# Two score tiles a quad shared between ScalarE and VectorE in the last full attention layer

## The chip, the cores and the metric

The kernel runs on one core of one Trainium2 chip. The metric is the device time of one execution in microseconds, the median of several runs. A profile of one execution shows what each engine did: TensorE (PE, its weight loads as PEld), VectorE (DVE), ScalarE (ACT), GpSimd (POOL) and the DMA queue of SyncE (SP).

## The reference

Four attention layers follow each other on x of 2048 rows by 512 columns, in float32. Layers 0 and 2 look back over a window of 256 rows, layers 1 and 3 over all rows; the two windowed layers have one set of weights, the two full ones another. Each layer is

```
x = x + attention(layernorm(x)) @ wo
```

with 32 heads of 16 columns. For a full layer:

```python
scores = jnp.einsum("bhqd,bhkd->bhqk", q, k) * Dh ** -0.5
p = softmax(scores, axis=-1)
o = jnp.einsum("bhqk,bhkd->bhqd", p, v)
```

So a full layer has 32 x 2048 x 2048 exponentials.

## The kernel before, in words

**Tiles.** Attention works on a quad: four heads and 512 queries (QC). In a full layer a quad goes through 16 steps j (NT), each of 128 keys, and in each step through two pairs of heads (pr). For one pair, `exps` (L755) issues eight matmuls of 64x32 array tiles that write a score tile `s` of 128 keys x 2 heads x 512 queries in PSUM, two banks, one for each head. The pool has two such tiles. One ScalarE instruction (L772) takes exp(SCALE x s) of both banks, 1024 elements a partition, into a tile `e` in SBUF, of which there are six. There is no maximum to subtract: a shift is worked into extra rows of queries and keys.

The function `pv` inside `attn_full` (L813) multiplies the exponentials with the values: four heads times two halves of the 128 keys (r), each half adding into its own accumulator bank `acc[r]`, head h in its partitions from 32 h on. The values carry a column of ones, so that row DH of an accumulator is the sum of the exponentials, by which `epilogue` (L718) divides. The profile lists two matmul records for each of these float32 matmuls.

**Order.** On PE and, in the full layers, on VectorE the order of the instructions is that in which the program emits them. ScalarE and GpSimd get theirs from the framework. `attention` (L1025) runs the generator `attn_full` and emits, for each step j: the scores and exponential of pair 0; then, at `flush(1)`, what waits in `pvq`, which is the value product of the step before the last; then the scores and exponential of pair 1; then, at `sd.step()`, a piece of side work. At the end of a quad the order differs: in step 0 of the next quad the value products of steps 14 and 15 are emitted, one after each pair, and the epilogue follows; step 1 has no value product.

Layer 3 runs over four groups t of eight heads, in each over four blocks c of 512 queries, in each over two quads: 32 quads. V is kept in tiles for half the heads and half the keys.

**Side work.** Projections of keys and queries (K3, Q3), values (VV) and the output projection (O3) of layer 3 run beside the attention in pieces of two matmul groups, dealt out by `Side.share` (L988). It keeps a budget, which grows with each step by the work that is left over the steps that are left, and a lag, which grows with PE time given to side work and falls by 0.42 a step. A piece is emitted if the lag is below 0.25 or the budget above 0.45. All is planned while the program is built, against a clock of its own (`spent`, `vec`); nothing of it happens on the chip. The results of side work come into one pair of PSUM banks and are joined on VectorE (`join`, L425). The squares of keys and queries are formed on GpSimd (L534) and summed on PE (L556).

**VectorE's queue.** Operations of VectorE that can wait go into four queues `VQ`, in order of precedence, and `drain` (L237) emits from the first that has something whenever the planned time of VectorE (`vt_`) is not ahead of the planner's clock by more than 0.2.

**Names that the change touches.** `PH`, the state of the phase (L212); `VQ` (L214); `exps` and its ScalarE instruction (L772); `attn_full` with `pv` (L805 to L820); and the loop in `attention` from L1059 to L1080. The tags "xh" (four buffers) and "st" (two buffers) belong to the normalisations, which have no work in layer 3.

Of the kernel before, what the change touches and what calls it, by code (L numbers as in the profile page):

```python
# [9 lines left out]
F32 = mybir.dt.float32  # L10
# [3 lines left out]
I32 = mybir.dt.int32  # L14
AF = mybir.ActivationFunctionType
ALU = mybir.AluOpType
AX = mybir.AxisListType

S, D, H, DH, WIN = 2048, 512, 32, 16, 256
P = 128  # L20
NT = S // P
# [3 lines left out]
QC = 512  # L25
# [5 lines left out]
SCALE = DH ** -0.5  # L31
MM = 0.222
HEAD_START = 100
PIECE = 4
EB, XB, XNB, WB, VB, OB = 6, 4, 4, 2, 3, 5
RINGS = WB, VB
L_MIN = 2.0 ** -90
L_SUM = 2.0 ** 60
WS = 16.0
W_MIN, W_MAX = 2.0 ** -7, 4.0  # L40


# [148 lines left out]
def fast_path(ctx, tc, flag, a_x, a_wqkv, a_wo, b_wqkv, b_wo, out):  # L191
# [3 lines left out]
    nc = tc.nc  # L195
# [3 lines left out]
    vp = pool("work", 2)  # L199
# [9 lines left out]
    mats = {(ty, s): layers[ty][1][:, s * D:(s + 1) * D] if s < 3 else layers[ty][2]  # L209
            for ty in range(2) for s in range(4)}  # L210

    XC, XN, V, O, OT, KM, PH = {}, {}, {}, {}, {}, {}, {"free": 0.0, "busy": False}  # L212
    WT, ST, pend = {}, {}, []
    VQ, vt_ = [deque() for _ in range(4)], [0.0]  # L214

    clock, DONE, XNR, ONR = [0.0], {}, {}, {}

    def spent(us):
        clock[0] += us
        return us  # L220
# [5 lines left out]
    def vec(us):  # L226

        vt_[0] = max(vt_[0], clock[0]) + us
# [39 lines left out]
    acc = [ps_c.tile([P, QC], F32, name=f"acc{i}") for i in range(2)]  # L268
# [52 lines left out]
    def split(ty, s, raw):  # L321

        w = wp.tile([P, NC, 2, D], F16, name=f"w{ty}_{s}", tag="vf", bufs=NQ)
        for k in range(NC):
            nc.scalar.activation(w[:, k, 0], raw[:, k], AF.Copy, scale=WS)
            nc.vector.scalar_tensor_tensor(w[:, k, 1], raw[:, k], WS, w[:, k, 0], op0=ALU.mult, op1=ALU.subtract)
            yield
# [96 lines left out]

    def join(dst, ps, scale=1 / WS):  # L425

        vec(1.4)
        nc.vector.tensor_scalar(dst, ps[0], scale, None, op0=ALU.mult)  # L428
        nc.vector.scalar_tensor_tensor(dst, ps[1], scale, dst, op0=ALU.mult, op1=ALU.add)  # L429
# [61 lines left out]
    def project(l, s, c, act, ht=None, ring=0):  # L491
# [13 lines left out]
        for t in range(NHT) if ht is None else (ht,):  # L505
# [5 lines left out]
            with tc.high_priority(HEAD_START):  # L511
# [4 lines left out]
                else:  # L516
                    sp = vp.tile([P, 2, QC], F16, name=f"sp{n}_{t}", tag="sp", bufs=3)
                    if act:
                        nc.scalar.activation(sp[:, 0], ps, AF.Copy, scale=1 / WS)
                    else:  # L520
                        nc.vector.tensor_scalar(sp[:, 0], ps, 1 / WS, None, op0=ALU.mult)
                    nc.vector.scalar_tensor_tensor(sp[:, 1], ps, 1 / WS, sp[:, 0], op0=ALU.mult, op1=ALU.subtract)
            full = PH["full"]
# [82 lines left out]
    def settle(all_=True):  # L606
        while pend and (all_ or pend[0][0] <= clock[0]):
            pend.pop(0)[1]()
# [143 lines left out]
        if u:  # L752
            soon(1, 1.2, parts)

    def exps(name, kt, qt, pr, pieces):  # L755

        ps = ps_s.tile([P, 2, QC], F32, name=f"s{name}", tag="s")
        w0 = min(p[3] for p in pieces)
        w1 = max(p[3] + p[2] for p in pieces)
        for kc, qc, wd_, s0 in pieces:  # L760
            if PH["full"]:
                for g in range(0, P, 32):
                    for h in range(2):
                        nc.tensor.matmul(ps[g:g + 32, h], kt[R * h:R * h + R, pr, kc + g:kc + g + 32],  # L764
                                         qt[R * h:R * h + R, pr], start=True, stop=True, skip_group_check=True)
                continue
            for h in range(2):
                nc.tensor.matmul(ps[:, h, s0:s0 + wd_], kt[R * h:R * h + R, pr, kc:kc + P],  # L768
                                 qt[R * h:R * h + R, pr, qc:qc + wd_], start=True, stop=True)
        spent(0.27)  # L770
        e = pp.tile([P, 2, QC], F32, name=f"e{name}", tag="e", bufs=EB)
        nc.scalar.activation(e[:, :, w0:w1], ps[:, :, w0:w1], AF.Exp, scale=SCALE)  # L772
        return e

    def flush(n):
# [27 lines left out]
        return kt, qt  # L803

    def attn_full(l, c, qd, kt, qt, a):  # L805
        for j in range(NT):
            es_ = []
            for pr in range(2):
                es_.append(exps(f"{l}_{c}_{qd}_{j}_{pr}", kt[j // 8], qt, pr, [(j % 8 * P, 0, QC, 0)]))
                if pr == 0:  # L810
                    yield None

            def pv(j=j, es_=es_):  # L813
                for h in range(4):
                    for r in range(2):
                        k = slice(R * r, R * r + R)
                        nc.tensor.matmul(acc[r][32 * h:32 * h + DH + 1, :], V[l, qd // 4, j // 8][k, j % 8, 4 * (qd % 4) + h, :],  # L817
                                         es_[h // 2][k, h % 2, :], start=(j == 0), stop=(j == NT - 1),
                                         skip_group_check=True)
            yield pv  # L820


# [99 lines left out]
    class Side:  # L922
# [13 lines left out]
        def one(self, force=False):  # L936

            drain()
            if PH["busy"]:
                return self.piece(PH["last"])  # L940
            if force:
                self.prefetch()
            at = [(w.ready_at(), i) for i, w in enumerate(self.q)]
            at = [(r, i) for r, i in at if r is not None]
            now = [i for r, i in at if r <= clock[0]]
            if now:
                i = now[0]
            elif force:
                r, i = min(at)
                clock[0] = r  # L950
            else:
                return None
            PH["last"] = self.q[i]
            return self.piece(PH["last"])
# [70 lines left out]
    def attention(l, works):  # L1025

        win = l % 2 == 0
        phase(l)
        load = load_win if win else load_full
        sd = None  # L1030
        for t in range(NHT if l == 3 else 1):
            for c in range(NQ):
                qds = range(2 * t, 2 * t + 2) if l == 3 else range(NQD)
                if l == 1:

                    sd = sd or Side(NT * NQD // 2, works[0], works[1], 0.33)
                    while ("Q", 1, c) not in DONE or pend and PH["busy"]:
                        sd.one(True)
                    settle()
                else:  # L1040
                    sd = Side((3 if win else NT) * len(qds), works[t * NQ + c], works[t * NQ + c + 1], 0.34 if l == 3 and t < 2 else 0.0)
                ahead = deque([PRE.pop("w", None) or load(l, c, qds[0])])
                if win:
                    ahead.append(load(l, c, 1))
                for qd in qds:
                    if (l, c, qd) == (1, 0, NQD // 2):
                        sd.finish()
                        sd = Side(NT * NQD * NQ - NT * NQD // 2, works[1], works[2], 0.33)
                    while (l, c, qd % 2) == (1, 0, 1) and qd + 1 in qds and ("S", 1, (qd + 1) // 2) not in DONE:
                        if ("K1", (qd + 1) // 2) in DONE and not PH["busy"]:  # L1050
                            settle()
                        else:
                            sd.one(True)
                    ops = ahead.popleft()
                    if qd + 1 + win in qds:
                        ahead.append(load(l, c, qd + 1 + win))
                    a = acc[qd % 2 if win else 0]
                    began, u = clock[0], 0
                    for f in (attn_win if win else attn_full)(l, c, qd, *ops, a):  # L1059
                        drain()  # L1060
                        if f is None:
                            flush(1)
                            if u == 1:
                                sd.step()
                            continue
                        clock[0] = max(clock[0], began + (2.4 if win else 1.8))
                        began = clock[0]
                        pvq.append([f])
                        if win:
                            flush(2)  # L1070
                            sd.step()
                            settle(False)
                        elif u == 0:
                            flush(1)
                        elif u:
                            sd.step()
                        while not win and (c, qd, u) == (0, 0, NT - 5) and ("V", l, 3, (0,), 2) not in DONE:
                            sd.one(True)
                        drain()
                        u += 1  # L1080
                    pvq[-1].append(lambda l=l, c=c, qd=qd, a=a: epilogue(l, c, qd, a))
                if l != 1 or c == NQ - 1:
                    sd.finish(l == 3 and (t, c) != (NHT - 1, NQ - 1))
                if not win and not PH["busy"]:
                    settle()
        flush(0)
        drain(4)
        phase(None)
# [151 lines left out]
    late = lambda l: [("N", l, 3)]  # L1240
# [56 lines left out]
```

## Time and profile before

| | |
|---|---|
| time, median of 3 runs | 2690.12 us (2688.55 to 2694.06) |
| time of the profiled execution | 2692.26 us |
| its span | 2690.2 us |
| ACT busy | 2363.6 us, 88% |
| PE busy | 2474.9 us, 92% |
| DVE busy | 1107.5 us, 41% |
| POOL busy | 531.8 us, 20% |
| exponentials, L772, of 128x1024 | 2368, mean 1066 ns |
| value products of the full layers, L817 | 16384 records, mean 590 ns |
| scores of the full layers, L764 | 16384 records, mean 381 ns |
| granted TensorE clock | 0.991 |

How to read it. Busy time counts an instruction from its start to its end, and instructions on one engine overlap: matmuls of different array tiles run at once and their ends are modelled, and an exponential begins before the one ahead of it has left the engine. So busy shares and mean durations are not rates. The rate at which an engine gets through its work is read from the starts of its instructions, in the timeline. A row of the timeline has the start, the duration, the engine, the line and operation, what is written from what with the shape, how many instructions are merged in it, and in brackets the idle time of the engine just before, with what ended it.

The first exponential of layer 3 starts at 1709.22 us, the last at 2669.2 us; from 1731.6 us on they follow each other with little idle time.

### The profile page before, as it was taken

What the parts mean: (1) busy time and instruction counts of PE and PEld (TensorE: products, weight loads), DVE (VectorE), ACT (ScalarE), POOL (GpSimd) and SP (SyncE); (2) the same over time, 40 slices, a digit from 0 to 9 for tenths busy, and PEclk for the clock granted to TensorE, in tenths of its full rate; (3) what the DMA queues carried; (4) which work ended last, traced back from release to release, by engine and by line L of the source; (5) the groups of instructions that cost most, each with busy time, mean ns of one, the idle gap of its engine ahead of it and who ended that gap; (6) DMA issues with size and microseconds to landing.
All of it is one profiled execution on the core that took longest, in us unless ns stands there. A gap on an engine that the chain in (4) does not pass through costs nothing.

```text
span 2690.2 us, 120844 instructions
## 1 busy us (share of the span) xinstructions
PE 2474.9 (92%) x54767; PEld 1133.5 (42%) x54767; DVE 1107.5 (41%) x2350; ACT 2363.6 (88%) x2671; POOL 531.8 (20%) x1072
## 2 busy tenths in 40 slices
PE   7889999999998999999999999899999999999997
PEld 3344444444443444444444444544444443433332
DVE  5576453223334434434236666232333323333333
ACT  4666764999999999999996776699999999999997
POOL 1556550000000100100116886010000000000000
PEclk9999999999999999999999999999999999999999
DMA  8889875232334325324227666433333323334332
GB/s 281 254 274 268 236 198 155 69 97 86 110 94 120 97 91 148 103 87 115 92 77 211 189 171 166 128 95 105 98 97 97 106 77 114 106 98 126 126 118 93
DMA packets 341189, 361.29 MB, mean 134 GB/s; under 512 B 117800, under 2 KB 256568, under 8 KB 334392
## 3 DMA queue, kind: packets, MB, share of 16 engines
q1 hardware_dynamic: 340664, 353.46, 44.2%
q8 instruction: 430, 7.05, 1.1%
q14 instruction: 95, 0.78, 0.1%
HBM read 240.65 MB, written 96.99 MB: 126 GB/s over the span
## 4 chain that ended last, share of the span: by engine, by line
ACT 55%; PE 23%; issue 11%; DVE 6%; DMA 3%; SPq 1%; POOL 0%; ACTq 0%; DVEq 0%; POOLq 0%
ACT e L772 55%; PE b L406 7%; PE acc L850 4%; PE acc L817 3%; PE s L764 2%; PE s L768 2%; PE bs L409 2%; PE b L409 2%; PE b L402 1%; DMA kt<-kw 1%; DVE xh L461 1%; DVE xn L455 0%; DMA qs<-sp 0%; SPq L483 0%; DVE xh L455 0%
## 5 line engine op out<-in xcount | busy, mean ns | idle before, releaser
L772 ACT ACTIVATE e<-s 128x1024 f32<-128x1024 f32 (+2 forms) x2432 | 2241.6, 1056 | 143.2 <-PE s L768 104.5
L817 PE MATMUL acc<-e,vt 64*17 64x512 f32 x16384 | 1094.6, 590 | 1.9 <-issue 1.9
L764 PE MATMUL s<-qt,kt 64*32 64x512 f16 x16384 | 860.0, 381 | 123.9 <-ACT e L772 97.1
L764 PEld LDWEIGHTS <-kt 64*32 64x32 f16 x16384 | 408.2, 89 | 935.1 <-issue 853.8
L817 PEld LDWEIGHTS acc<-e,vt 64*17 64x17 f32 x16384 | 283.8, 92 | 67.9 <-issue 8.1
L843 POOL TENSOR_SCALAR_AFFINE_SELECT e<-e 128x256 f32<-128x256 f32 x512 | 230.5, 457 | 154.8 <-ACT e L772 154.1
L840 POOL TENSOR_SCALAR_AFFINE_SELECT e<-e 128x256 f32<-128x256 f32 x448 | 201.5, 456 | 96.5 <-ACT e L772 93.2
L850 PE MATMUL acc<-e,vt 128*17 128x384 f32 (+2 forms) x2816 | 202.6, 390 | 2.5 <-POOL e L840 2.2
L749 POOL TENSOR_TENSOR oh<-o,oh 128x512 f16<-128x512 f32 x31 | 36.1, 1165 | 725.1 <-DVE oh L748 725.1
L428 DVE TENSOR_SCALAR sa<-acc 128x512 f32<-128x512 f32 x64 | 44.3, 691 | 291.3 <-PE acc L817 291.3
L406 PE MATMUL b<-xc,w 128*32 128x512 f16 x2496 | 152.4, 389 | 10.8 <-DVE km L575 6.9
L714 DVE SCALAR_TENSOR_TENSOR x<-b,x 128x512 f32<-128x512 f32 x122 | 84.0, 689 | 175.1 <-PE b L402 168.4
L534 POOL TENSOR_TENSOR sq_h<-sp_h 128x512 bf16<-128x512 f16 x29 | 43.0, 1483 | 562.4 <-DVE sp_h L528 562.4
L768 PE MATMUL s<-qt,kt 64*128 64x384 f16 (+2 forms) x1408 | 120.8, 276 | 28.2 <-ACT e L772 22.7
L534 POOL TENSOR_TENSOR sq<-sp 128x512 bf16<-128x512 f16 x32 | 45.8, 1434 | 496.8 <-DVE sp L528 473.6
L402 PE MATMUL b<-xc,w 64*32 64x512 f16 x3072 | 126.4, 376 | 1.5 <-DVE j L429 0.8
L428 DVE TENSOR_SCALAR vt<-b 128x256 f32<-128x256 f32 (+1 forms) x36 | 18.4, 512 | 233.8 <-PE b L402 219.9
L402 PE MATMUL b<-wo,oh 64*32 64x512 f16 x2592 | 109.1, 376 | 4.1 <-DVE m_None L591 1.8
L402 PE MATMUL b<-xc,w_h 64*32 64x512 f16 x2784 | 111.8, 376 | 0.1
L428 DVE TENSOR_SCALAR j_h<-b 128x512 f32<-128x512 f32 x29 | 20.1, 692 | 214.6 <-PE b L402 214.6
L406 PEld LDWEIGHTS <-w 128*32 128x32 f16 x2496 | 73.5, 99 | 79.2 <-issue 27.7
L768 PEld LDWEIGHTS <-kt 64*128 64x128 f16 x1408 | 52.2, 94 | 125.7 <-issue 105.3
(142 smaller groups left out, 1942.3 us busy)
## 6 DMA issues: line engine op xcount, KB each, us to landing
kt<-kf SPq DMA_DIRECT2D x128, 512.0 KB
qt<-qs SPq DMA_DIRECT2D x128, 256.0 KB
xd<-x SPq DMA_DIRECT2D x96, 256.0 KB
x<-xd SPq DMA_DIRECT2D x96, 256.0 KB
w<-wd SPq DMA_DIRECT2D x21, 1024.0 KB
kt<-kw SPq DMA_DIRECT2D x64, 256.0 KB
qs<-sp SPq DMA_DIRECT2D x48, 256.0 KB
wo<-wd SPq DMA_DIRECT2D x12, 1024.0 KB
```

The source lines that it names most:

```text
L402: nc.tensor.matmul(ps[g:g + 32, r], a[k, g:g + 32], b[k], start=(i == 0), stop=(i == len(pairs) - 1), skip_group_check=True)
L406: nc.tensor.matmul(ps[g:g + 32], a[:, g:g + 32], b, start=(i == 0), stop=(i == len(pairs) - 1), skip_group_check=True)
L409: nc.tensor.matmul(ps, a, b, start=(i == 0), stop=(i == len(pairs) - 1))
L534: nc.gpsimd.tensor_tensor(sq, sp[:, 0], sp[:, 0], ALU.mult)
L714: nc.vector.scalar_tensor_tensor(xs[i], p, 1 / WS, xs[i], op0=ALU.mult, op1=ALU.add)
L764: nc.tensor.matmul(ps[g:g + 32, h], kt[R * h:R * h + R, pr, kc + g:kc + g + 32], qt[R * h:R * h + R, pr], start=True, stop=True, skip_grou ...
L768: nc.tensor.matmul(ps[:, h, s0:s0 + wd_], kt[R * h:R * h + R, pr, kc:kc + P], qt[R * h:R * h + R, pr, qc:qc + wd_], start=True, stop=True)
L772: nc.scalar.activation(e[:, :, w0:w1], ps[:, :, w0:w1], AF.Exp, scale=SCALE)
L817: nc.tensor.matmul(acc[r][32 * h:32 * h + DH + 1, :], V[l, qd // 4, j // 8][k, j % 8, 4 * (qd % 4) + h, :], es_[h // 2][k, h % 2, :], star ...
L840: nc.gpsimd.affine_select(v, v, pattern=[[0, 2], [-1, P]], compare_op=ALU.is_gt, fill=0.0, base=0, channel_multiplier=1)
L843: nc.gpsimd.affine_select(v, v, pattern=[[0, 2], [1, P]], compare_op=ALU.is_ge, fill=0.0, base=0, channel_multiplier=-1)
L850: nc.tensor.matmul(a[32 * h:32 * h + DH + 1, q * P:(q + nb) * P], V[l, (4 * c + j) // 4][:, j % 4, 4 * qd + h, :], es_[h // 2][:, h % 2, s ...
```

## The change

In layer 3 alone, the second pair's score tile of steps j = 4 and j = 9 of each quad is shared by two engines. ScalarE takes the exponential of one bank; the other bank (bank 1 in step 4, bank 0 in step 9: `OWN`) goes to VectorE. `own_exp` reads it from PSUM, scaled to a power of two in fixed point, splits it by two bit operations into an integer and a fractional part, and evaluates a polynomial of five `scalar_tensor_tensor` steps, in float32 tiles with the tag "xh". The framework is told that the two reads of the tile need no order between them. The first operation is emitted at once; the seven others go into a new fifth queue of VectorE, `VQ[4]`, the last in precedence.

The result is twice the exponential, so the values of these two heads and key tiles are halved, on GpSimd, at the start of each quad (`vh`, tag "st"). The value product of a shared head is left out of its step's `pv`, and the products of both shared heads are emitted together by `late`, four matmuls, after the second pair's scores of step 15, ahead of that step's side work. Before them `late` emits whatever is left in `VQ[4]`. The planner counts 0.86 for them on its clock and on the lag.

```diff
+OWN = {4: 1, 9: 0}
+POLY = (-0.2122642642036666, 20.582234973412888, 57.43304580516819, 188.4105936388931, 265.3878017523131)
+OWN_AT = 13
+LEAD, LOW = 0x40000000 | 0x761904, -117.0
...
-    VQ, vt_ = [deque() for _ in range(4)], [0.0]
+    VQ, vt_ = [deque() for _ in range(5)], [0.0]
...
+    def own_exp(name, s, got, other):
+        u, e, p = (vp.tile([P, QC], F32, name=f"{n}{name}", tag="xh", bufs=XNB) for n in ("ou", "oe_", "op_"))
+        ui, ei = u.bitcast(I32), e.bitcast(I32)
+        with tc.high_priority(HEAD_START):
+            x = nc.vector.tensor_scalar(ui, s, SCALE * 1.4426950408889634 * 2.0 ** 23, LOW * 2.0 ** 23, op0=ALU.mult, op1=ALU.max)
+            tc.declare_no_dep(x.ins, other.ins, reason="the two read different banks")
+        vec(0.75)
+        ops = [(0.45, lambda: nc.vector.tensor_scalar(ei, ui, 0x7F800000, LEAD, op0=ALU.bitwise_and, op1=ALU.bitwise_xor)),
+               (0.45, lambda: nc.vector.tensor_scalar(ui, ui, 0x7FFFFF, 0x3E800000, op0=ALU.bitwise_and, op1=ALU.bitwise_or))]
+        for i, k in enumerate(POLY):
+            ops.append((0.7, lambda i=i, k=k: nc.vector.scalar_tensor_tensor(p, p if i else u, k / 4.0 ** (i + 1), e if i == 4 else u,
+                                                                            op0=ALU.add, op1=ALU.mult)))
...
+        for us, f in ops:
+            VQ[4].append((clock[0] + 0.6, us, lambda f=f: one(f)))
+        return p
...
-        nc.scalar.activation(e[:, :, w0:w1], ps[:, :, w0:w1], AF.Exp, scale=SCALE)
+        if own is not None:
+            x = nc.scalar.activation(e[:, 1 - own], ps[:, 1 - own], AF.Exp, scale=SCALE)
+            got[name] = own_exp(name, ps[:, own], got, x)
+        else:
+            nc.scalar.activation(e[:, :, w0:w1], ps[:, :, w0:w1], AF.Exp, scale=SCALE)
...
     def attn_full(l, c, qd, kt, qt, a):
+        got = {} if l == 3 else None
+        if l == 3:
+            vh = [vp.tile([P, 4, 6], F32, name=f"vh{l}_{c}_{qd}_{x}", tag="st").rearrange("p a b -> p (a b)")[:, :DH + 1] for x in range(2)]
+            for x, (j, own) in enumerate(OWN.items()):
+                nc.gpsimd.tensor_scalar(vh[x], V[l, qd // 4, j // 8][:, j % 8, 4 * (qd % 4) + 2 + own, :], 0.5, None, op0=ALU.mult)
...
+                mine = OWN if l == 3 else {}
+                for h in range(4):
+                    if j not in mine or h != 2 + mine[j]:
+                        head(j, h, es_[h // 2][:, h % 2], j == NT - 1)
+                def late():
+                    while got["left"]:
+                        vec(VQ[4][0][1])
+                        VQ[4].popleft()[2]()
+                    for x, (i, own) in enumerate(mine.items()):
+                        head(i, 2 + own, got[f"{l}_{c}_{qd}_{i}_1"], False, vh[x])
+                    spent(0.86)
+                if j == OWN_AT and mine:
+                    PH["late"] = late
...
                         elif u:
+                            if PH["late"]:
+                                PH["late"]()
+                                PH["late"] = None
+                                sd.lag += 0.86
                             sd.step()
```

`head(j, h, e, last_, v)` issues the two matmuls (one for each half of the keys) of head h, as `pv` did before. `OWN_AT` is 13 because the `pv` of step 13 is emitted in step 15.

More of the change, by code (lines that the diff above doesn't have):

```diff
@@ L210, in fast_path @@
             for ty in range(2) for s in range(4)}
-    XC, XN, V, O, OT, KM, PH = {}, {}, {}, {}, {}, {}, {"free": 0.0, "busy": False}
+    XC, XN, V, O, OT, KM, PH = {}, {}, {}, {}, {}, {}, {"free": 0.0, "busy": False, "late": None}
     WT, ST, pend = {}, {}, []
-    VQ, vt_ = [deque() for _ in range(4)], [0.0]
+    VQ, vt_ = [deque() for _ in range(5)], [0.0]
     clock, DONE, XNR, ONR = [0.0], {}, {}, {}
@@ L753, in epilogue, with one, exps @@
             soon(1, 1.2, parts)
-    def exps(name, kt, qt, pr, pieces):
+    def own_exp(name, s, got, other):
[10 more added lines that the diff above has]
+                                                                            op0=ALU.add, op1=ALU.mult)))
+        got["left"] = got.get("left", 0) + len(ops)
+        def one(f):
+            f()
+            got["left"] -= 1
+        for us, f in ops:
+            VQ[4].append((clock[0] + 0.6, us, lambda f=f: one(f)))
+        return p
+    def exps(name, kt, qt, pr, pieces, own=None, got=None):
         ps = ps_s.tile([P, 2, QC], F32, name=f"s{name}", tag="s")
@@ L808, in attn_full @@
             for pr in range(2):
-                es_.append(exps(f"{l}_{c}_{qd}_{j}_{pr}", kt[j // 8], qt, pr, [(j % 8 * P, 0, QC, 0)]))
+                own = OWN.get(j) if l == 3 and pr else None
+                es_.append(exps(f"{l}_{c}_{qd}_{j}_{pr}", kt[j // 8], qt, pr, [(j % 8 * P, 0, QC, 0)], own, got))
                 if pr == 0:
@@ L813, in pv, with head @@
             def pv(j=j, es_=es_):
-                for h in range(4):
+                def head(j, h, e, last_, v=None):
+                    v = V[l, qd // 4, j // 8][:, j % 8, 4 * (qd % 4) + h, :] if v is None else v
                     for r in range(2):
                         k = slice(R * r, R * r + R)
-                        nc.tensor.matmul(acc[r][32 * h:32 * h + DH + 1, :], V[l, qd // 4, j // 8][k, j % 8, 4 * (qd % 4) + h, :],
-                                         es_[h // 2][k, h % 2, :], start=(j == 0), stop=(j == NT - 1),
-                                         skip_group_check=True)
+                        nc.tensor.matmul(acc[r][32 * h:32 * h + DH + 1, :], v[k], e[k], start=(j == 0), stop=last_, skip_group_check=True)
+                mine = OWN if l == 3 else {}
[11 more added lines that the diff above has]
+                    PH["late"] = late
             yield pv
```

## The prediction

> **What bounds the kernel now.** I read the page's head and chain first, then the window of the second full layer, which is all that the change touches.
>
> ```profile
> span 2690.2 us, 120844 instructions
> PE 2474.9 (92%) x54767; PEld 1133.5 (42%) x54767; DVE 1107.5 (41%) x2350; ACT 2363.6 (88%) x2671; POOL 531.8 (20%) x1072
> ACT 55%; PE 23%; issue 11%; DVE 6%; DMA 3%; SPq 1%; POOL 0%; ACTq 0%; DVEq 0%; POOLq 0%
> ```
> ```profile
> 1731.60:2670.00 938.40, 856.78 (x21280) 379.20 (x21271) 309.18 (x580) 924.83 (x1003) 57.51 (x42) 1.00 0.35 104
> ```
> The columns of the window are its length, then PE, PEld, DVE, ACT and POOL busy, clock, DMA. ACT is busy 924.83 of 938.40 us, so the layer looks like 32 quads of 32 exponentials, one after another, on a full ScalarE. If that were all, shorter exponentials would be time won. The starts of single exponentials say otherwise. First, two stretches of ACT alone, merged:
>
> ```profile
> 2407.25 4.69 ACT L772 ACTIVATE e<-s 128x1024 f32<-128x1024 f32 x5
> ...
> 2419.10 13.01 ACT L772 ACTIVATE e<-s 128x1024 f32<-128x1024 f32 x14
> ```
> An exponential that follows another lasts 1.08 to 1.09 us in the record and overlaps its successor. Taking 1.08 from the first row leaves four intervals of (4.69 - 1.08) / 4 = 0.90 us: ScalarE's own pace. The second row gives (13.01 - 1.09) / 13 = 0.917. ScalarE is held back by 0.013 us an exponential though no idle time shows, since gaps under 0.17 us vanish in the overlap. Now the rows of both engines across the end of a quad. ACT:
>
> ```profile
> 2401.60 1.08 ACT L772 ACTIVATE e<-s 128x1024 f32<-128x1024 f32 x1
> 2402.51 1.09 ACT L772 ACTIVATE e<-s 128x1024 f32<-128x1024 f32 x1
> 2403.43 1.08 ACT L772 ACTIVATE e<-s 128x1024 f32<-128x1024 f32 x1
> 2404.35 1.09 ACT L772 ACTIVATE e<-s 128x1024 f32<-128x1024 f32 x1
> 2405.27 1.08 ACT L772 ACTIVATE e<-s 128x1024 f32<-128x1024 f32 x1
> 2406.18 1.09 ACT L772 ACTIVATE e<-s 128x1024 f32<-128x1024 f32 x1
> 2407.25 1.02 ACT L772 ACTIVATE e<-s 128x1024 f32<-128x1024 f32 x1
> ```
> and PE:
>
> ```profile
> 2402.74 0.41 PE L764 MATMUL s<-qt,kt 64*32 64x512 f16 x8 [0.35 <-ACT e L772]
> 2402.95 1.05 PE L817 MATMUL acc<-e,vt 64*17 64x512 f32 x16
> 2403.81 0.41 PE L764 MATMUL s<-qt,kt 64*32 64x512 f16 x8
> 2404.02 0.63 PE L402 MATMUL b<-xc,w_h 64*32 64x512 f16 x16
> 2404.57 0.41 PE L764 MATMUL s<-qt,kt 64*32 64x512 f16 x8
> 2404.78 1.05 PE L817 MATMUL acc<-e,vt 64*17 64x512 f32 x16
> 2405.64 0.41 PE L764 MATMUL s<-qt,kt 64*32 64x512 f16 x8
> 2405.86 1.05 PE L817 MATMUL acc<-e,vt 64*17 64x512 f32 x16
> 2406.71 0.41 PE L764 MATMUL s<-qt,kt 64*32 64x512 f16 x8
> ```
> There are two score tiles. The scores of 2402.74 start 0.06 us after the exponential of 2401.60 ends (2402.68) and gives its tile back. They take PE 0.21, the value product behind them 0.86 (2402.95 to 2403.81), and only then can the next scores start. Those of 2403.81 are read at 2404.35: 0.54 us from start of scores to start of exponential. The same 0.54 stands at 2405.64 to 2406.18 and at 2406.71 to 2407.25, so there ScalarE starts the moment its scores are ready. The first scores of each pair have room: 2402.74 + 0.54 = 2403.28, started 2403.43. So the pace is set by a **loop**: exponential 1.08, return 0.06, scores 0.21, value product 0.86, scores to exponential 0.54, altogether 2.75 us from the first exponential of a pair to the second of the next pair (2401.60 to 2404.35). At the quad's end two value products come in a row, and the exponential of 2407.25 follows its predecessor by 1.07 instead of 0.90.
>
> **The change part by part.** *ScalarE.* 64 exponentials (two a quad, 32 quads) lose half their columns.
>
> ```profile
> L772 ACT ACTIVATE e<-s 128x512 f32<-128x512 f32 x32 | 18.0, 598 | 5.3 <-PE s L768 5.2
> ```
> This is the same line on 128x512 in the windowed layers. A 128x1024 that waited took 1.02 (2407.25), so 0.42 us goes from each, 64 x 0.42 = 27 us of ScalarE work. How much reaches the end? Let the exponential of 2402.51 be the shared one. ScalarE is free at 2402.51 + 0.90 - 0.42 = 2402.99. The next scores cannot be ready before 2403.28, since their tile comes back from 2401.60's exponential as before; it starts 0.15 earlier than 2403.43. The one after waits for the scores of 2403.81, behind the value product: 2404.35, as now. Gain there: none. The room of 0.15 that the other half of the loop got lets ScalarE run at 0.90 for some pairs (0.01 to 0.02 each) before the loop closes on it again. Bounds per shared tile: 0 and 0.15; I take 0.05, nearer to the rows of the waiting exponentials: -3 us (0 to -10).
>
> *The late product on PE.* The shared heads' products leave their steps (j = 4 and 9, numbering the key steps of a quad from 0) and are issued together in step 15, behind its second scores. Do the six products left take less than eight?
>
> ```profile
> 2360.37 0.39 PE L556 MATMUL b<-sq_h,hsum 64*32 64x512 bf16 x2 [1.51 <-DVE m L591]
> 2360.38 0.60 PE L764 MATMUL s<-qt,kt 64*32 64x512 f16 x8
> ```
> Two matmuls on two of the eight array tiles start at 2360.37, eight scores 0.01 later, and these last 0.60 instead of 0.41: their last columns wait a full 0.2 us for those two tiles. So a group costs its depth, not its number. Six of eight products still take 0.86, and the four late ones 0.86 more. The bounds are that and half (0.43, with 0.21 back from each thinned step); I take 0.86. "TensorEngine Tiling (Array Packing)" of the Trainium skill, Key Properties, says that different tiles can execute in parallel; the two rows agree, and by it the depth counts too. Put 0.86 behind the scores of 2403.81: it runs 2404.02 to 2404.88. With no side work there, the scores of 2404.57 start at 2404.88 (exponential 2405.42, +0.15); value product to 2405.95; scores of 2405.64 at 2405.95 (exponential 2406.49, +0.31); scores of 2406.71 at 2407.02, exponential 2407.56, **+0.31 us a quad**, 32 x 0.31 = +9.9. The change adds 0.86 to the planner's lag, which keeps side work away from that step unless the budget is above 0.45. Where it lets some in (16 matmuls of 2404.02, 0.43 to the next row), the quad pays 0.43 more; I take five quads of 32, +2.2 (bounds 0 and 32, +14). Against that the place is as full now as it can be, and nothing hides the late product.
>
> *VectorE.* Per shared tile one read of a bank, two mask operations and five steps of the polynomial.
>
> ```profile
> L428 DVE TENSOR_SCALAR sa<-acc 128x512 f32<-128x512 f32 x31 | 21.4, 692 | 120.4 <-PE acc L817 120.4
> L529 DVE TENSOR_TENSOR sp_h<-j_h,sp_h 128x512 f16<-128x512 f32 x26 | 18.0, 692 | 0.9
> L528 DVE CAST sp_h<-j_h 128x512 f16<-128x512 f32 x26 | 11.1, 427 | 1.9 <-DVE j_h L429 0.4
> ```
> 0.69 + 2 x 0.43 + 5 x 0.69 = 5.0 us, 64 times 320 us on top of 309.18 in 938.40: two thirds busy, not a bound by itself. What matters is the read, which now also releases the tile. Scores of 2401.97 (2402.51 - 0.54) are ready at 2402.5, the read ends at 2403.2; the tile is wanted at 2403.81. Room 0.6. One running operation (at most 0.69, now every third moment) hides in it; two in a row, one in nine, would cost about 0.5: 7 x 0.5, and the planner spaces them, so +1 (bounds 0 and 64 x 0.69 = 44 if every read met a full operation beyond the room). Queued behind a waiting read on VectorE are the joins that free the side work's bank; they have the planner's 2 us of room. The polynomial of step 9 has five steps of 1.83 us before the late product needs it, against 5.0 us of work.
>
> *GpSimd.* Two halvings of 128x17 a quad, 64 in all.
>
> ```profile
> L843 POOL TENSOR_SCALAR_AFFINE_SELECT e<-e 128x256 f32<-128x256 f32 x512 | 230.5, 457 | 154.8 <-ACT e L772 154.1
> ```
> At most 0.46 each by this nearest row, on an engine busy 57.51 of 938.40 us, and not needed for 27 us: nothing. If that cover went, 64 x 0.46 = 29 us of POOL could delay the squares alone. "SBUF — State Buffer" of the Trainium skill, Who interferes with whom, says that a DVE operation with two SBUF inputs and a GpSimd operation that reads SBUF shut each other out, and the polynomial has five such a tile. The trace has no squares on GpSimd away from VectorE's work to test it; by it the squares of the side work come later, which is the third rival's case and is in its chance. No DMA is added or moved, SP's queue is untouched.
>
> **Sum.** +9.9 + 2.2 - 3 + 1 = +10 us. The profiled execution took 2692.3 (span 2690.2 and 2.1 around it), the median of the runs is 2690.1, 2.2 less. So 2702 by the profiled run's scale, and 2700 by the median's, which I predict.
>
> **Rivals.** *First, faster: ScalarE is the limit after all.* For it: 924.83 of 938.40 us busy and ACT's 55% of the chain. Then all 27 us come off, less a third for waits: 2663 to 2672. "TensorEngine Tiling (Array Packing)", PSUM Bottleneck, speaks for it: use both ScalarE and VectorE to empty PSUM; the rows of the loop show what it leaves out here, that PE cannot refill sooner. Chance 0.10. *Second, no change.* The late product costs half (tiles by number, not depth): 2404.02 + 0.43 is before 2404.57, so it vanishes, and the thinned steps shorten the loop by 0.21 twice a quad; or the gain is near its upper bound, -10 against +9.9. 2685 to 2695. Against it: the rows of 2360. Chance 0.25. *Third, much slower: the late product waits for the polynomial.* It is last in the planner's queues, so whatever is left of it is forced out just ahead of the product, and PE then stands 0.7 us for each operation left, with ScalarE behind it. It decides from about one left operation a quad: 32 x 0.7 = +22 on top, 2722. Squares that come late on GpSimd end here too. Against it: 5.0 us in five steps of 1.83. Chance 0.12. *Fourth, the readers stay ordered* though the change says not: the read would start when the half exponential ends, 2402.51 + 0.60, end at 2403.85, and hold up scores wanted at 2403.81 by about 0.1: 64 x 0.1, 2706. Chance 0.08, and on the same side as the forecast, which has the remaining 0.45.
>
> **How the numbers follow.** About 0.2%, or 5.4 us, is what a measurement of this kernel can tell from no change. Slower: 0.45 + 0.12 + 0.08 = 0.65; same 0.25; faster 0.10. The forecast's own range is 2696 to 2709, from the bounds of side work and gain. The range for 8 in 10 leaves out the first rival and most of the third: 2686 to 2714.
>
> **What would show it.** Right: the interval of the exponential after the two value products at a quad's end stays near 1.07 while the two before it grow to about 1.07, with the late products as 8 records between them; the exponential after a shared tile starts some 0.77 us behind it, and the next lies over 1.0 behind that, so the pair gains next to nothing. Wrong: quads below 29.3 us, two intervals of 0.5 and 0.9 around a shared tile, a late group of 0.43, or PE waiting there on VectorE.

## The result, and the profile after

| | median | ratio to before | 95% interval |
|---|---|---|---|
| before | 2689.34 us | | |
| changed | 2775.04 us | 1.0316 | 1.0297 to 1.0335 |

The change makes the kernel 3.2% slower, 86 us. The forecast was 2700, its range ended at 2714: the direction was right, the size was not. All ratios here compare executions at the usual speed; one of the four of e2_plan_only, below, took 5238.6 us and is in its median but not in its ratio.

The head, the busy times and the chain of the page after:

```profile
span 2776.6 us, 121486 instructions
PE 2512.9 (91%) x54767; PEld 1154.8 (42%) x54767; DVE 1439.1 (52%) x2862; ACT 2355.6 (85%) x2671; POOL 547.4 (20%) x1136
ACT 46%; PE 33%; issue 10%; DVE 6%; DMA 4%; POOL 1%; SPq 0%; ACTq 0%; DVEq 0%; POOLq 0%
```

VectorE gained 332 us of work (320 were worked out) and ACT's share of the chain went to PE. From the first exponential of layer 3 to its last it is now 1043.8 us, before it was 959.9: 83.9 of the 86 us lie there.

The waits of ACT and of PE in layer 3, after (who waited for whom: us in total, times, longest us):

```profile
ACT e L802 <- PE s L790: 93.2, 45, 16.1
...
PE s L790 <- ACT e L802: 54.3, 148, 1.0
PE s L790 <- DMA qt<-qs: 40.0, 7, 11.6
PE b L560 <- DVE m L595: 9.1, 6, 1.6
```

and the same row of ACT before:

```profile
ACT e L772 <- PE s L764: 17.5, 20, 1.7
```

The wait of the scores for a load of queries (`qt<-qs`), up to 11.6 us at once, was 0.9 us in all before. The prediction has no such wait. The six of them that take more than 1 us stand at the end of a block of queries. One in the timeline after, at the end of the last block of the first eight heads:

```profile
1962.02 0.41 PE L790 MATMUL s<-qt,kt 64*32 64x512 f16 x8
1962.25 0.38 PE L560 MATMUL b<-sq_h,hsum 64*32 64x512 bf16 x2
1962.26 1.03 PE L855 MATMUL acc<-op,vh 64*17 64x512 f32 x8
1963.44 1.22 DVE L579 TENSOR_REDUCE km<-b 32x1 f32<-32x1024 f32 x1 [3.91 <-PE acc L855]
...
1964.71 0.39 PE L560 MATMUL b<-sq_h,hsum 64*32 64x512 bf16 x2 [1.42 <-DVE km L579]
1964.87 0.34 DVE L623 TENSOR_SCALAR mk<-ones,kx 32x512 f16<-32x512 f16 x1
1965.24 0.29 SPq L628 DMA_DIRECT2D kf<-mk  x1
...
1967.19 0.68 DVE L594 TENSOR_SCALAR m<-b 32x512 f16<-32x512 f32 x1 [1.97 <-DMA kf<-mk]
1967.90 0.68 DVE L595 SCALAR_TENSOR_TENSOR m<-b,m 32x512 f16<-32x512 f32 x1
1968.62 0.28 SPq L607 DMA_DIRECT2D qs<-m  x1
...
1970.63 0.87 SPq L817 DMA_DIRECT2D qt<-qs  x2
1976.49 0.63 PE L790 MATMUL s<-qt,kt 64*32 64x512 f16 x8 [11.38 <-DMA qt<-qs]
1976.87 1.95 PE L855 MATMUL acc<-e,vt 64*17 64x512 f32 x16
1977.24 1.02 ACT L802 ACTIVATE e<-s 128x1024 f32<-128x1024 f32 x1 [13.60 <-PE s L790]
```

Read it from the top. Behind the block's last scores PE sums the squares of keys and of queries (L560), one after the other, since both use the one bank and VectorE must read it in between. From the sums come the shifts: that of the keys is written to memory (`kf<-mk`), that of the queries waits for that write, is formed and written (`qs<-m`), and only then can the next block's queries be loaded (`qt<-qs`). ScalarE stands still for 13.6 us. The queries' part of that chain, for the same block, before:

```profile
1928.70 0.40 PE L556 MATMUL b<-sq_h,hsum 64*32 64x512 bf16 x2
1929.13 0.68 DVE L590 TENSOR_SCALAR m<-b 32x512 f16<-32x512 f32 x1 [2.85 <-PE b L556]
...
1930.56 0.28 SPq L603 DMA_DIRECT2D qs<-m  x1
1931.87 0.89 SPq L787 DMA_DIRECT2D qt<-qs  x2
```

There it ran in the middle of a quad, a good ten steps ahead of the block's end near 1951, and nobody waited. So the question was why the squares come late now. In the code the rule is in `Side.share`: squares that are due (in `pend`) are emitted only if the planner's clock has reached `vt_[0] - 0.2`, the time up to which VectorE is planned to be busy. And `drain` fills VectorE's plan from the queues until it is more than 0.2 ahead. While the new fifth queue holds polynomial steps, the plan is kept ahead, and the squares are passed over, step after step, until the block's end forces them.

### The profile page after: what moved, and what is told of

The parts are those of the page before. It is cut to its first block, busy times and chain, and to the rows that moved or that the text cites. A ratio compares the mean times of both kernels' runs of the same rounds, so it can differ in the third digit from the quotient of the medians.

```text
span 2776.6 us, 121486 instructions
## 1 busy us (share of the span) xinstructions
PE 2512.9 (91%) x54767; PEld 1154.8 (42%) x54767; DVE 1439.1 (52%) x2862; ACT 2355.6 (85%) x2671; POOL 547.4 (20%) x1136
## 4 chain that ended last, share of the span: by engine, by line
ACT 46%; PE 33%; issue 10%; DVE 6%; DMA 4%; POOL 1%; SPq 0%; ACTq 0%; DVEq 0%; POOLq 0%
ACT e L802 45%; PE b L410 8%; PE acc L855 8%; PE s L790 5%; PE acc L900 4%; PE b L406 3%; PE s L794 2%; PE bs L413 1%; PE b L413 1%; DMA qt<-qs 1%; DMA x<-in_A_x_dram 1%; DMA qs<-m 1%; DVE xh L465 1%; DVE xn L459 0%; DMA kt<-kw 0%
## 5 line engine op out<-in xcount | busy, mean ns | idle before, releaser
L802 ACT ACTIVATE e<-s 128x1024 f32<-128x1024 f32 (+2 forms) x2368 | 2202.3, 1047 | 239.3 <-PE s L794 111.3
L855 PE MATMUL acc<-e,vt 64*17 64x512 f32 x16128 | 1113.6, 595 | 0.0
L790 PE MATMUL s<-qt,kt 64*32 64x512 f16 x16384 | 893.4, 383 | 158.0 <-ACT e L802 92.6
L855 PEld LDWEIGHTS acc<-e,vt 64*17 64x17 f32 x16128 | 295.7, 93 | 75.3 <-issue 10.0
L770 DVE SCALAR_TENSOR_TENSOR op<-op,ou 128x512 f32<-128x512 f32 x192 | 138.4, 721 | 5.3
L406 PE MATMUL b<-xc,w 64*32 64x512 f16 x3072 | 126.1, 376 | 1.5 <-DVE j L433 0.8
L432 DVE TENSOR_SCALAR j<-b 128x512 f32<-128x512 f32 x32 | 22.0, 688 | 200.8 <-PE b L406 200.8
L406 PE MATMUL b<-xc,w_h 64*32 64x512 f16 x2784 | 123.5, 377 | 0.0
L406 PE MATMUL b<-wo,oh 64*32 64x512 f16 x2592 | 116.2, 379 | 5.6 <-DVE m_None L595 1.8
L718 DVE SCALAR_TENSOR_TENSOR x<-b,x 128x512 f32<-128x512 f32 x122 | 83.9, 688 | 64.6 <-PE b L406 61.6
L840 POOL TENSOR_SCALAR vh<-vt 128x17 f32<-128x17 f32 x64 | 15.8, 263 | 498.3 <-PE acc L855 470.9
```

Of the source, the lines that this page charges most:

```text
L406: nc.tensor.matmul(ps[g:g + 32, r], a[k, g:g + 32], b[k], start=(i == 0), stop=(i == len(pairs) - 1), skip_group_check=True)
L718: nc.vector.scalar_tensor_tensor(xs[i], p, 1 / WS, xs[i], op0=ALU.mult, op1=ALU.add)
L770: ops.append((0.7, lambda i=i, k=k: nc.vector.scalar_tensor_tensor(p, p if i else u, k / 4.0 ** (i + 1), e if i == 4 else u, op0=ALU.add, ...
L855: nc.tensor.matmul(acc[r][32 * h:32 * h + DH + 1, :], v[k], e[k], start=(j == 0), stop=last_, skip_group_check=True)
```

## The experiments

Theory A: that rule, in the planner, costs some 75 of the 86 us, and what remains is the cost that the prediction worked out. Rival B: the work that was added on the chip costs them, by a loaded VectorE or by a late product that waits for the polynomial.

**e1_squares_go.** The changed kernel with one condition of the planner altered:

```diff
-            if pend and not PH["busy"] and clock[0] >= max(PH["free"], pend[0][0], vt_[0] - 0.2):
+            if pend and not PH["busy"] and clock[0] >= max(PH["free"], pend[0][0], 0.0 if VQ[4] else vt_[0] - 0.2):
```

> The changed kernel, but the planner may emit the sums of squares on PE although VectorE's planned time lies ahead, as long as the polynomial's queue is not empty. No operation is added or taken away. Theory A (the polynomial fills VectorE's planned time, so the squares wait for the end of a block of queries, the query shift is written there, and the next block's load waits for it): the stalls of 7 to 17 us at the ends of blocks go; 2700 to 2712 us, layer 3's quads near 29.6 us. Rival B (VectorE's 320 us of added work, or the late product waiting for it, costs the time): 2765 us or more, as before this edit.

Measured: 2702.32 us, ratio 1.0041 (1.0027 to 1.0055). 73 us go with an edit that takes no operation away. ACT's waits for scores in layer 3:

```profile
ACT e L802 <- PE s L790: 16.9, 28, 1.7
```

No wait for a load of queries is left in the view. A holds, B falls for these 73 us.

**e2_plan_only.** The kernel before, with entries in the planner and nothing behind them:

```diff
+                if l == 3 and pr and j in (4, 9):
+                    vec(0.75)
+                    for us in (0.45, 0.45, 0.7, 0.7, 0.7, 0.7, 0.7):
+                        VQ[4].append((clock[0] + 0.6, us, lambda: None))
...
+                            if PH["late"]:
+                                PH["late"]()
+                                PH["late"] = None
+                                sd.lag += 0.86
```

Here `late` empties the fifth queue and counts 0.86 on the clock, no more.

> The kernel before, with nothing of the change on the chip: only the planner's entries are made, seven empty operations in a fifth queue and their planned times at steps 4 and 9 of layer 3, and 0.86 on clock and lag at step 15. Every instruction is one of the kernel before; their order is the changed kernel's. Theory A: 2690 + 60 to 80 us, 2750 to 2770, with waits of the score matmuls for the query load at ends of blocks. Rival B: within 10 us of 2690.

Measured: 2765.5 us, ratio 1.0253 (1.0226 to 1.0280). The waits of its PE and ACT in layer 3:

```profile
PE s L764 <- DMA qt<-qs: 47.7, 7, 12.0
...
ACT e L772 <- PE s L764: 86.1, 32, 15.4
```

Seven waits for a load of queries again, as in the changed kernel, with not one instruction of the change on the chip; in the two traces the sums of squares stand at the same places among the scores. This is the same result from the other side.

**e9_plan_mended.** e2_plan_only with the edit of e1_squares_go.

> e2_plan_only (no operation of the change on the chip) with the edit of e1_squares_go in the planner. If the wait of the squares for VectorE's planned time is the whole of e2's loss: within 5 us of the kernel before. If the planned times of the late product or the lag cost something by themselves: 10 us or more above it.

Measured: 2687.75 us, ratio 0.9979 (0.9969 to 0.9988). All of e2's loss goes. It ends a little below the kernel before. There PE waited five times, 7.5 us in all, with squares that were due, for VectorE to read the sums ahead of them (`m<-b`); here once, 1.5 us. ACT's waits for scores in layer 3 are 11.9 us in 15, against 17.5 in 20. e9 and e1 have the same plan (their sums of squares stand at the same places too), one without and one with the change's work, so their ratios give that work's cost: 1.0041 / 0.9979 = 1.0062, 17 us. It is this that the prediction had worked out, as 10. The next runs take it apart.

**e3_half_only.** ScalarE's part alone, on the kernel before; the value products of the heads left out go with it:

```diff
+        if own is not None:
+            nc.scalar.activation(e[:, 1 - own], ps[:, 1 - own], AF.Exp, scale=SCALE)
...
+                    if l == 3 and (j, h) in ((4, 3), (9, 2)):
+                        continue
```

> The kernel before, with ScalarE's exponential of one bank left out in the second pair of steps 4 and 9 of layer 3, and with it the value products of that head and key tile (left out of the sums). Nothing on VectorE or GpSimd, no late product. If the loop over scores and value product sets the pace, as the prediction has it: 0 to 10 us below the kernel before, some 3. If ScalarE is the limit: 27 us below.

Measured: 2686.0 us, ratio 0.9979 (0.9967 to 0.9992): 6 us, not 27. From the starts of the exponentials, a quad without stalls takes 29.29 us where it took 29.42: 0.065 a shared tile, where some 0.4 were taken from ScalarE.

**e7_late_alone.** PE's part alone, on the kernel before: the same products taken out of their steps, and four matmuls put behind the second scores of step 15.

```diff
+                    if l == 3 and (j, h) in ((4, 3), (9, 2)):
+                        continue
...
+                            nc.tensor.matmul(acc[r][32 * h:32 * h + DH + 1, :], V[l, qd // 4, i // 8][k, i % 8, 4 * (qd % 4) + h, :],
+                                             es_[1][k, h % 2, :], start=False, stop=False, skip_group_check=True)
```

> The kernel before, with the value products of one head in steps 4 and 9 of layer 3 taken out of their steps and four matmuls of the same shape issued behind the second scores of step 15 (they take step 13's exponentials, so the sums are others). Planner untouched. Depth rule of the prediction: 0.31 us a quad where no side work stands there and up to 0.86 where it does, 10 to 18 us above the kernel before. If cost goes by number: within 3 us.

Measured: 2707.43 us, ratio 1.0063 (1.0041 to 1.0085), 15.5 us. A quad without stalls takes 29.72 us (29.42 + 0.30), five others 30.16 (29.42 + 0.74). Steps 4 and 9 have two matmuls less here too, and the 0.30 are the forecast's 0.31 with no gain from them: so e3's gain is put down to the shorter exponential.

**e4_no_late.** e1_squares_go without those matmuls (`head(...)` in `late` replaced by `pass`).

> As e1_squares_go, without the four late matmuls a quad: the shared heads' two key tiles are left out of the sums. The plan is the same. If the late product costs its full depth at the quad's end: 0.31 x 32 = 10 us less than e1_squares_go, and the two intervals ahead of the quad's end go back from 1.07 to 0.92. If it costs half or waits for the polynomial: no difference, or over 20 us.

Measured: 2682.88 us, ratio 0.9972 (0.9962 to 0.9981), 19 us less than e1_squares_go, where 10 were expected. The lengths of quads, from one first exponential to the next, say why: without stalls 29.29 us against 29.59 in e1_squares_go, 0.30 as expected, but seven of e1's quads take about 30.03, that is 0.74 more. All seven have side work beside the late product.

**e5_no_poly.** e1_squares_go with the polynomial taken off VectorE and its planned times kept:

```diff
+        ops, p = [(us, f if n == 1 else lambda: None) for n, (us, f) in enumerate(ops)], u
```

> As e1_squares_go, with one of the two mask operations and the five polynomial steps left out (the late product takes the masked bits for the exponentials): VectorE loses 64 x 4.1 = 265 us of work, the plan is the same. Theory A: within 4 us of e1_squares_go. Rival B: 20 us or more below it.

Measured: 2700.29 us, ratio 1.0038 (1.0025 to 1.0050), 2 us from e1_squares_go, within its interval. VectorE's 265 us are hidden, but for a few us at most: one quad of e5's trace takes 35.19 us where e1's takes 30.58, for a reason that the profile does not show, and without it e5's layer 3 would be some 4 us shorter than e1's.

**e6_ordered.** By an oversight this kernel was built from e1_squares_go, not from the changed kernel as its expectation says; so it is compared with e1.

```diff
-            tc.declare_no_dep(x.ins, other.ins, reason="the two read different banks")
```

> The changed kernel with the framework's own order between the two readers of a shared tile (the declaration left out). The prediction's fourth rival priced it at 0.1 us a tile, 64 x 0.1 = 6 us above the changed kernel. If the readers are ordered already: no difference.

Measured: 2714.38 us, ratio 1.0087 (1.0067 to 1.0108), 12 us above e1_squares_go; in quads without stalls 29.88 us against 29.59, 0.15 a shared tile, where 0.1 had been worked out. In its trace each of VectorE's 64 reads starts after the half exponential beside it has ended; in e1_squares_go and in the changed kernel all 64 start before that end. So there the two engines do read without an order.

**e8_no_side_there.** e1_squares_go with no side work dealt out in step 15:

```diff
                                 sd.lag += 0.86
+                                sd.k += 1
+                                sd.prefetch()
...
+                            if not continue_:
+                                sd.step()
```

> As e1_squares_go, with no side work dealt out in step 15, where the late product stands (it comes in other steps). If the late product costs 0.30 us in a quad without side work beside it and 0.74 with it, the quads of 30.0 us go to 29.6 us: some 13 quads x 0.43, about 5 us below e1_squares_go. If the cost has nothing to do with side work: no difference. It does not beat the kernel before under either.

Measured: 2726.16 us, ratio 1.0121 (1.0104 to 1.0137): 24 us more (22 by the ratios), not 5 less. Six of the seven quads did what was expected, 29.59 where e1 had 30.03. But the side work that lost its place did not fit elsewhere. Other quads grew, so that layer 3 takes 972.6 us from its first exponential to its last, e1_squares_go 967.9. And behind the last exponential, at 2680.2 and 2680.7, e8's span ends at 2724.5 and e1's at 2703.2: output projections that were carried from block to block are done alone at the end. The window behind the last exponential, in e8 and in e1_squares_go (length, then PE, PEld, DVE, ACT, POOL busy, clock, DMA):

```profile
2681.00:2724.00 43.00, 18.46 (x218) 5.58 (x213) 19.07 (x38) 0.29 (x1) 0.00 (x0) 0.61 0.43 131
```
```profile
2681.00:2703.00 22.00, 7.58 (x54) 2.09 (x34) 8.00 (x22) 0.82 (x1) 0.00 (x0) 0.69 0.18 64
```

218 matmuls stand in that end, 172 of them of output projections in pieces (L406), where 54 stood and none of these. So one step in sixteen less for side work costs more than it saves.

No run with the whole of the change's work beats the kernel before. e9_plan_mended does, by 0.2%, and has none of that work; e3 and e4 are below it by 0.2 and 0.3%, and leave products out of the sums.

## Why the prediction was wrong, point by point

**The loop that sets the pace: right.** ScalarE's starts around a shared tile in the changed kernel:

```profile
1987.18 1.07 ACT L802 ACTIVATE e<-s 128x1024 f32<-128x1024 f32 x1
1988.08 0.66 ACT L799 ACTIVATE e<-s 128x512 f32<-128x512 f32 x1
1988.84 1.03 ACT L802 ACTIVATE e<-s 128x1024 f32<-128x1024 f32 x1
1989.92 1.02 ACT L802 ACTIVATE e<-s 128x1024 f32<-128x1024 f32 x1
```

The exponential after the shared one starts 0.76 behind it (forecast 0.77), and the next 1.08 behind that (over 1.0): ScalarE is done early and waits for scores. 56 of the 64 shared tiles in e1_squares_go have these two intervals, 0.76 and 1.07. The gain, e3's 6 us, was forecast as 3 with bounds 0 and 10. Two readings were a little off: ScalarE is held back by 0.917 - 0.903 = 0.014 us an exponential, not 0.013, and the half exponential took 0.66 us, not the 0.60 of the windowed layers.

**The late product: right in kind, too small in sum.** The end of a quad without side work, in e1_squares_go, PE and then ACT:

```profile
2621.02 0.41 PE L790 MATMUL s<-qt,kt 64*32 64x512 f16 x8
2621.26 1.03 PE L855 MATMUL acc<-op,vh 64*17 64x512 f32 x8
...
2622.12 0.39 PE L790 MATMUL s<-qt,kt 64*32 64x512 f16 x4
```
```profile
2620.64 1.08 ACT L802 ACTIVATE e<-s 128x1024 f32<-128x1024 f32 x1
2621.56 1.09 ACT L802 ACTIVATE e<-s 128x1024 f32<-128x1024 f32 x1
2622.62 1.02 ACT L802 ACTIVATE e<-s 128x1024 f32<-128x1024 f32 x1
2623.69 1.02 ACT L802 ACTIVATE e<-s 128x1024 f32<-128x1024 f32 x1
```

Eight records of four matmuls, and the last four of the next scores start 2622.12 - 2621.26 = 0.86 behind them: depth, not number. The intervals 1.06 and 1.07 are the forecast's. 0.30 a quad was measured (0.31), and 0.74 with side work beside it (0.31 + 0.43). The row that the prediction gave for the 0.43 shows 0.55 (2404.02 to 2404.57); the 0.43 itself came out, 30.03 - 29.59 = 0.44. The mis-sized term is "five quads of 32": in e1's trace side work (L406) stands within 1 us of the late product in sixteen. 32 x 0.30 + 16 x 0.44, the second an upper bound, is 16.6 us; the late product cost 19 where 9.9 + 2.2 stood, and the rest, some 2, is within the noise of the two runs.

**VectorE on the chip: right.** e5 gives 2 us for the polynomial within the interval of e1. For the reads the forecast had +1: quads without stalls take 29.29 us in e4, which has the reads, and in e3, which has not. Most of the mask operations took the 0.43 us of the forecast.

**The step that failed** is in that part on VectorE, where the reads were hidden "and the planner spaces them, so +1", and at the end of the part on GpSimd, "No DMA is added or moved". The effect of the new queue on the planner's other work was put at nothing, without a reason. The prediction counted VectorE's load on the chip and took the planner's queues as a service. But VectorE's planned time is also a condition for other work. Squares were emitted only when it was not ahead, the fifth queue kept it ahead, and with the squares moved VectorE's shifts, the write of `qs<-m` and the load of `qt<-qs` behind it. That cost some 73 of the 86 us. e2_plan_only shows that this alone costs 2.5%, without an instruction of the change; e1_squares_go and e9_plan_mended show that one condition brings it back. That the forecast had the right direction rests on the other 17 us; for these 73 it was luck. The third rival (late squares, +22 and more) had the size of the right order and the wrong cause: neither GpSimd's time nor a waiting late product made them late. PE's waits for the polynomial and for the halved values are small in the changed kernel:

```profile
PE acc L855 <- DVE op L770: 1.6, 3, 1.0
...
PE acc L855 <- POOL vh L840: 1.0, 2, 0.5
```

**The rule of shut-out** between VectorE and GpSimd ("SBUF — State Buffer" of the Trainium skill, Who interferes with whom): the traces agree with it, but it is VectorE that waits, where the prediction had the squares wait. A square on GpSimd and the step of the polynomial beside it, in e1_squares_go:

```profile
2042.16 1.54 POOL L538 TENSOR_TENSOR sq_h<-sp_h 128x512 bf16<-128x512 f16 x1 [10.60 <-DVE sp_h L532]
```
```profile
2042.73 1.53 DVE L770 SCALAR_TENSOR_TENSOR op<-op,ou 128x512 f32<-128x512 f32 x1
```

The step takes 1.53 us instead of 0.69. So do 14 of the 320 steps there, each beside a square that had started before it, and ten mask operations take 1.27 us instead of 0.43 beside an operation of GpSimd that had started before them. That makes 24 x 0.84 = 20 us of VectorE's time; the steps' part of it is in the load that e5_no_poly shows to be hidden. The squares themselves took 1.54 us each in e1_squares_go and 1.54 in e5_no_poly without the five steps of two inputs, after 1.48 before. No run shows where these 0.06 us come from.

What stays open is small. The ratios of e9, e4 and e1 give 2 us less for the change's work without the late product, which is within the noise, and 19 for that product; the sum, 17, is the cost of the work on the chip. Of the remaining 73 some 12 are an estimate of PE's slow time behind the six waits (below): eleven intervals between exponentials of about 2.13 us there, against 1.07.

## What to carry to other kernels

Before costing a shortened operation, look at the starts on its engine: if some of them fall exactly one fixed delay behind the producer, the engine paces nothing there, however full it looks. In a kernel with a planner of its own, read every condition in which a planned time stands before adding entries to it: work that is hidden on the chip can still hold back other work in the plan. And to tell the plan from the work, run the old instructions in the new order, and the new ones in the old.

## What the hardware showed that was not expected

After each of the six stalls PE comes back at half its clock. The window behind the stall of 13.6 us, and the one that follows (length, then PE, PEld, DVE, ACT, POOL busy, clock, DMA):

```profile
1976.50:1982.20 5.70, 5.70 (x80) 2.02 (x88) 1.04 (x2) 2.74 (x3) 0.00 (x0) 0.50 0.01 4
```
```profile
1982.25:1987.00 4.75, 4.25 (x112) 1.74 (x104) 3.22 (x9) 4.63 (x6) 0.00 (x0) 1.00 0.15 59
```

The granted clock is 0.50 for 5.7 us; the value product at 1976.87 takes 1.95 instead of 1.05, and two intervals between exponentials take 2.13 us instead of 1.07. So this stall costs about 2 us more than it lasts. "TensorE: Matmul & The Clock Gate" of the Trainium skill, Part 1: The HAM clock gate, states that the array runs at half its clock after an idle window and returns after some 3.4 us of sustained work. The trace agrees with the first; the return took 5.7 us of work here, not 3.4. The prediction had no stall long enough for it.
